# A two-layer attention and SwiGLU kernel: output projection over 448 rows in place of 512, and the second projection's banks, buffers and order

## The chip, the cores and the metric

The kernel runs on one core of a Trainium2 chip. The metric is the device time of one execution in microseconds (us), taken as the median of several runs. The core's engines appear in the profile as PE (the matmul engine, TensorE), PEld (its weight loads), DVE (VectorE), ACT (ScalarE), POOL (GpSimd) and SP (SyncE, which here only issues DMAs). A trailing q, as in SPq, is an engine's queue of DMA issues.

## The reference

Sequence length 2048, model width D = 448, 16 query heads of 28, one key and value head shared by all of them, and a feed-forward width of 1792. The same weights are used in both layers.

```python
def _A_ref(x, wq, wk, wv, wo):
    q = (x @ wq).reshape(B, S, 16, 28).transpose(0, 2, 1, 3)
    k = x @ wk
    v = x @ wv
    p = softmax(einsum("bhqd,bkd->bhqk", q, k) * 28 ** -0.5)
    o = einsum("bhqk,bkd->bhqd", p, v)
    return o.transpose(0, 2, 1, 3).reshape(B, S, 448) @ wo

def _B_ref(x, w_gate, w_up, w_down):
    return (silu(x @ w_gate) * (x @ w_up)) @ w_down

x = x + _A_ref(layernorm(x));  x = x + _B_ref(layernorm(x))   # layer 0
x = x + _A_ref(layernorm(x));  x = x + _B_ref(layernorm(x))   # layer 1
```

All inputs and the output are float32.

## The kernel before

**Precision.** Nearly every product of weights and activations is made in three matmuls: each operand is split into a rounded high part and the rest (names that end in h and l), and hi x hi, hi x lo and lo x hi are summed in PSUM. `split(h, l, r)` does it on POOL: L135 writes the high part and L136 the rest.

**Tiling.** The 2048 tokens are 4 chunks of 512, and a chunk has 4 token tiles of 128. The residual stream `xres` stays in SBUF. The 16 heads are 4 groups g of 4; in a group each head has 32 partitions, 28 used and 4 spare.

**Projection.** An object for the layer walks through 16 products (chunk c, slice m of the q, k, v weights), numbered by `seen`. Each is a run of matmuls into one PSUM bank (L312) that `bank(...)` deals out in the order of a tuple: before, `ALL` is banks 4 to 7 and then 0 to 3. ACT copies the bank to a stage buffer (L531), and SP sends that to DRAM (`qd`, `kt`), from where heads are read back in another layout. `plan[n, k]` lists what is written into the program around product n: for layer 0, the layer norm of the next chunk. A norm is, per token tile, BN statistics and their aggregate on DVE (L217, L218), for the chunk one reciprocal root on POOL (`scale`, L222 and L223), and per token tile the scaled rows on DVE (L230) with a copy on POOL (L232); PE flips those rows (L248) into the layout of the products. `maxima(c)` makes, with 4 matmuls (L439), a transposition (L441), a reduction and further small DVE steps, bounds on the scores of chunk c, which are taken off before the exponential. In the second layer the normed rows of chunks 0 to 2 come turned, by way of DRAM, and are split by ACT (L292) and DVE (L293, L302); chunk 3 is normed here (`ready`).

**Attention loop.** 128 cycles m in each layer; 8 of them (u = 0 to 7) make one (chunk, head group) i. A cycle has on PE the scores of two key tiles, y0 and y1 (L597): for each tile 3 passes of 4 matmuls with 32 rows, for j = 0 to 3 the heads of the group. j < 3 goes to three banks side by side (`three`), j = 3 to a single bank (`bank`). ACT takes the exponential of `three` (L619), DVE copies `bank` to a buffer `pair` (L618), and ACT takes the exponential of both tiles' copies at once (L620). Then PE makes P-V for the cycle before (L652) into the single bank of y0, and DVE adds it to an accumulator (L661). `singles` alternates banks 6 and 7 between y0 and y1.

**After the last cycle of a group**, `post` sends the sums of the exponentials (a row of ones in V gives them as the 29th row of each head) to `rs` (L675). `rest`, written into cycle m + 4, takes their reciprocals, sends them to DRAM and back as a broadcast (L686), and POOL multiplies (L693) and splits the result into `onh` and `onl`.

**Output projection.** `on` holds a chunk's four groups of 128 partitions, so the contraction is over 512 rows, 448 of them used; the weights `woh`, `wol` have the same layout, with zeros in the spare rows. When the last group of a chunk is through, 48 matmuls (4 token tiles x 4 groups x 3 parts, L582) are written behind cycle u = 6 of the next group, tiles 1, 2, 3 into the banks of `three` and tile 0 into a single bank, with an add to `xres` for each (L586): three adds behind tile 3 and one behind tile 0. This happens for chunks 0, 1 and 2 inside the loop, six times in all; for chunk 3 it stands behind the loop, among the first matmuls of the feed-forward part (`unit`, L332).

**Order.** Each engine takes its own instructions in the order in which the program was written. So where a piece is written (the tables `plan`, `due` and `aside`, and the place in `scores`) sets the order of every queue; engines wait for each other by semaphores. POOL also splits feed-forward weights (`weights`, L130 to L136 and L159) that are loaded in cycles u = 4 of groups 11 to 14. A slower variant of the whole (`full=True`) stands in a branch that is not taken with these inputs.

## Time and profile before

| | |
|---|---|
| median of 3 runs | 1984.87 us (1984.5 to 1985.03) |
| profiled execution | 1986.38 us, its span 1984.7 us |
| PE busy | 1960.1 us, 99% |
| ACT busy | 1270.1 us, 64% |
| DVE busy | 968.9 us, 49% |
| POOL busy | 555.3 us, 28% |
| mean granted TensorE clock | 0.996 |

The span is the time from the first to the last instruction of the profiled execution; the rest of its time lies around it. A row of a timeline gives the start in us from the span's start, the duration, the engine, the line and operation, out<-in, shapes and the number of equal instructions put together; in brackets is the idle time of the engine ahead of it, and what ended that. A row of the waits reads: engine and work, what it waited for, us in total, number of times, longest. A row of the chain of waits has the start, the length and the work. A row of a window gives its length, then busy time and instructions of PE, PEld, DVE, ACT and POOL, the granted clock (1 is full), the DMA engines' share and GB/s. Matmuls are pipelined: the step from one start to the next is what a matmul costs PE, and its own duration is longer. In the names, a trailing number of a buffer is left out.

Layer 0's projection lies at 9 to 70 us, its attention loop after that to about 540 us, the feed-forward part to 1001 us; the second projection at 1001 to 1054 us, with the second layer's attention and feed-forward behind it.

### The profile page before, as it was taken

What the parts mean: (1) busy time and instruction counts of PE and PEld (TensorE: products, weight loads), DVE (VectorE), ACT (ScalarE), POOL (GpSimd) and SP (SyncE); (2) the same over time, 40 slices, a digit from 0 to 9 for tenths busy, and PEclk for the clock granted to TensorE, in tenths of its full rate; (3) what the DMA queues carried; (4) which work ended last, traced back from release to release, by engine and by line L of the source; (5) the groups of instructions that cost most, each with busy time, mean ns of one, the idle gap of its engine ahead of it and who ended that gap; (6) DMA issues with size and microseconds to landing.
All of it is one profiled execution on the core that took longest, in us unless ns stands there. A gap on an engine that the chain in (4) does not pass through costs nothing. (4 is left out here: it accounts for less than half of the span.)

```text
span 1984.7 us, 43786 instructions
## 1 busy us (share of the span) xinstructions
PE 1960.1 (99%) x18469; PEld 1337.4 (67%) x18469; DVE 968.9 (49%) x1638; ACT 1270.1 (64%) x1888; POOL 555.3 (28%) x597
## 2 busy tenths in 40 slices
PE   9999999999999999999999999999999999999998
PEld 7544545445468999999974445454454789988886
DVE  6656565665743223222665565656657432222222
ACT  4899797997953333333348997979979433333332
POOL 5222113122214333333331221122221242333320
PEclk9999999999999999999999999999999999999999
DMA  5101011021030011110241010200211301011102
GB/s 165 54 23 33 18 36 39 19 54 31 24 84 26 17 32 32 32 32 22 79 134 35 26 31 12 62 12 23 51 48 26 74 17 32 17 31 32 32 1 76
DMA packets 99875, 80.50 MB, mean 41 GB/s; under 512 B 25848, under 2 KB 82296, under 8 KB 99672
## 3 DMA queue, kind: packets, MB, share of 16 engines
q1 hardware_dynamic: 98120, 76.44, 14.2%
q8 instruction: 146, 2.39, 0.5%
q10 hardware_dynamic: 1552, 1.20, 0.2%
q14 instruction: 57, 0.47, 0.1%
HBM read 56.24 MB, written 20.58 MB: 39 GB/s over the span
## 5 line engine op out<-in xcount | busy, mean ns | idle before, releaser
L619 ACT ACTIVATE pt<-three 128x1536 f32<-128x1536 f32 x512 | 714.9, 1449 | 65.7 <-PE three L597 62.4
L652 PE MATMUL bank<-pt,vsb 128*32 128x512 f32 x3072 | 490.8, 598 | 1.9 <-DVE pair L618 1.2
L652 PE MATMUL bank<-pair,vsb 128*32 128x512 f32 x1024 | 487.4, 598 | 0.5 <-ACT pair L620 0.5
L597 PE MATMUL bank<-qstack,keys 32*128 32x512 f32 x1536 | 471.9, 426 | 1.7 <-DVE xres L586 1.7
L332 PE MATMUL bank<-xh,wgh 64*128 64x512 f32 x1728 | 448.7, 389 | 0.0
L597 PE MATMUL three<-qstack,keys 32*128 32x512 f32 x4608 | 430.4, 409 | 2.5 <-ACT stage L531 2.5
L597 PEld LDWEIGHTS three<-qstack,keys 32*128 32x128 f32 x4608 | 262.8, 183 | 232.2 <-issue 203.0
L618 DVE COPY pair<-bank 128x512 f32<-128x512 f32 x512 | 353.8, 691 | 100.7 <-PE bank L597 71.6
L332 PE MATMUL bank<-xh,wgl 64*128 64x512 f32 x1404 | 370.3, 390 | 0.0
L332 PE MATMUL bank<-xl,wgh 64*128 64x512 f32 x1296 | 336.5, 389 | 0.0
L332 PE MATMUL bank<-wdh,h 64*128 64x448 f32 x1792 | 333.6, 363 | 1.7 <-ACT h L945 0.8
L944 DVE TENSOR_TENSOR sg<-bank,sg 128x512 f32<-128x512 f32 x112 | 77.4, 691 | 502.8 <-ACT sg L943 498.6
L332 PEld LDWEIGHTS bank<-xh,wgh 64*128 64x128 f32 x1728 | 265.7, 184 | 16.6 <-issue 1.3
L652 PEld LDWEIGHTS bank<-pt,vsb 128*32 128x32 f32 x3072 | 101.7, 109 | 253.2 <-issue 153.2
L620 ACT ACTIVATE pair<-pair 128x1024 f32<-128x1024 f32 x256 | 271.8, 1062 | 0.0
L597 PEld LDWEIGHTS bank<-qstack,keys 32*128 32x128 f32 x1536 | 245.1, 184 | 37.0 <-DVE o L659 5.2
L827 POOL TENSOR_TENSOR xres<-stage,xres 128x448 f32<-128x448 f32 x108 | 127.3, 1197 | 502.8 <-ACT stage L826 502.5
L332 PEld LDWEIGHTS bank<-wdh,h 64*128 64x128 f32 x1792 | 247.3, 184 | 15.2 <-issue 2.0
L661 DVE TENSOR_TENSOR o<-bank,o 128x512 f32<-128x512 f32 x224 | 154.7, 691 | 209.1 <-PE bank L652 209.1
L339 ACT COPY seen<-bank 128x1 f32<-128x1 f32 x664 | 82.1, 163 | 250.6 <-PE bank L332 247.6
L332 PEld LDWEIGHTS bank<-xh,wgl 64*128 64x128 f32 x1404 | 218.7, 184 | 14.1
L332 PE MATMUL bank<-wdl,h 64*128 64x448 f32 x896 | 221.1, 367 | 0.0
(133 smaller groups left out, 2120.9 us busy)
## 6 DMA issues: line engine op xcount, KB each, us to landing
o<-rd SPq DMA_DIRECT2D x32, 256.0 KB
qd<-stage SPq DMA_DIRECT2D x32, 224.0 KB
qraw<-qd SPq DMA_DIRECT2D x128, 56.0 KB
wdr<-in_B_w_down_dram SPq DMA_DIRECT2D x28, 224.0 KB
xt<-tb SPq DMA_DIRECT2D x24, 224.0 KB
wr<-in_B_w_gate_dram SPq DMA_DIRECT2D x28, 192.0 KB
wr<-in_B_w_up_dram SPq DMA_DIRECT2D x28, 192.0 KB
xn<-xt SPq DMA_DIRECT2D x6, 768.0 KB
```

Source lines behind the costliest of these rows:

```text
L332: nc.tensor.matmul(po, a, b, start=start, stop=stop, skip_group_check=True)
L339: nc.scalar.copy(seen[:, i : i + 1], po[:, 0:1])
L597: nc.tensor.matmul(three[:, j, :] if j < 3 else one, k[js, kp, ks], q[js, part, :], start=(z == 0), stop=(z == 2), tile_position=(32 * j, 0),)
L618: copies.append(nc.vector.tensor_copy(pt1, one))
L619: es.append(nc.scalar.activation(pt, threes[y], AF.Exp, scale=SCALE))
L620: es.append(nc.scalar.activation(pair, pair, AF.Exp, scale=SCALE))
L652: nc.tensor.matmul(to[32 * j : 32 * j + 32, :], vsb[:, n % NT, :], pts[n][j], start=(y == 0), stop=(y == 1), skip_group_check=True,)
L661: f = nc.vector.tensor_tensor(accs[i][:, 0, :], to, accs[i][:, 0, :], ALU.add)
L827: nc.gpsimd.tensor_tensor(r, s, r, ALU.add)
L944: nc.vector.tensor_tensor(in_order(sg, sq), natural(pg[1], sq), in_order(sg, sq), ALU.mult)
```

## The change

It has several parts.

1. **448 rows.** Heads 2 and 3 of group 0 (56 rows of the contraction) are moved into the 4 spare partitions of the other groups' heads (3 groups x 16 spare partitions = 48) and of group 0's own heads 0 and 1 (8). Groups 1 to 3 are then full, and group 0 has 64 rows. That half group is stored twice, in partitions 0 to 63 and in 64 to 127, so that two token tiles can use the two halves of the array side by side. `load_wo` loads the weights into this layout with 32 DMAs a layer in place of 8, and POOL's two zero fills go.
2. **Projection.** 36 matmuls over 128 rows for groups 1 to 3 and 12 over 64 rows, as 6 pairs: tiles 1 and 2, then 3 and 0. All four adds stand behind, in the order 1, 2, 3, 0. Behind the loop the pairs are tiles 0 and 1, then 2 and 3.
3. **Moving the rows.** `post` gives three pieces. `rest` (cycle m + 4) ends with the product on POOL. `spread` (m + 5) moves rows with DMAs on SP: for group 0, two writes to DRAM, two reads and one copy of the half group; for the others four reads of 4 rows. `parts` (m + 6, or m + 7 for group 0) does the split into `onh` and `onl`. The sums are sent with one DMA in place of four. For the last group of all, `rest` is written ahead of `unit(0, 0, 0)`, `spread` behind it, then the fetch of weights, then `parts`.
4. **Score order.** For even tiles (y0) the matmuls of a pass go j = 3, 0, 1, 2.
5. **Layer 0's projection.** The statistics and the root of chunks 2 and 3 are made together, ahead of chunk 2's scaled rows; POOL's root takes 8 columns.
6. **Second projection.** Its banks go round in the order 0 to 7; chunk 3's raw products use slices of a spare tile `xn` in place of two stage buffers; the norm of chunk 3 is applied behind product 5 in place of product 8.
7. **Last maxima.** Everything behind the transposition is written one cycle later.

The core of the diff:

```diff
-        fs = [lambda t=t: stat(t) for t in range(4)] + [scale]
+        fs = [lambda t=t: stat(t) for t in range(4 * chunks)] + [scale]
...
-            raw = self.pool.tile([P, 512], F32, name="stage")
+            if self.layer and c == NC - 1:
+                if "xn" not in self.spare:
+                    self.spare["xn"] = pers.tile([P, 4, 512], F32, name="xn")
+                raw = self.spare["xn"][:, self.seen % 4, :]
+            else:
+                raw = self.pool.tile([P, 512], F32, name="stage")
...
-            wide.append(ALL)
+            wide.append((0, 1, 2, 3, 4, 5, 6, 7) if self.layer else ALL)
...
+                    for g in (2 * z, 2 * z + 1):
+                        s_ = r[:, g % 2, :]
+                        if g == 0:
+                            for half in (0, 64):
+                                for q in range(2):
+                                    p0 = half + 32 * q
+                                    nc.sync.dma_start(s_[p0 : p0 + DH, :], wo[DH * q : DH * q + DH, :])
+                                    n0 = 4 * DH - 8 + 4 * q
+                                    nc.sync.dma_start(s_[p0 + DH : p0 + 32, :], wo[n0 : n0 + 4, :])
+                            continue
+                        own = wo[4 * DH * g : 4 * DH * g + 4 * DH, :]
+                        n0 = 2 * DH + 16 * g - 16
+                        for q in range(4):
+                            nc.sync.dma_start(s_[32 * q : 32 * q + DH, :], own[DH * q : DH * q + DH, :])
+                            nc.sync.dma_start(s_[DH + q :: 32, :], wo[n0 + 4 * q : n0 + 4 * q + 4, :])
                     zs = slice(2 * z, 2 * z + 2)
...
+                def passes(c):
+
                     oh, ol = on[c]
-                    ts_ = slice(P * t, P * t + P)
+                    return (oh, woh), (oh, wol), (ol, woh)
+
+                def add_to(c, t, po):
+
+                    return lambda: nc.vector.tensor_tensor(
+                        xres[:, 4 * c + t, :], po[:, 0:D], xres[:, 4 * c + t, :], ALU.add
+                    )
+
+                def full_rows(c, t, po, gs):
+
                     for g in gs:
-                        for z, (a, b) in enumerate(((oh, woh), (oh, wol), (ol, woh))):
+                        for z, (a, b) in enumerate(passes(c)):
                             nc.tensor.matmul(
-                                po[:, 0:D], a[:, g, ts_], b[:, g, :], start=(g + z == 0), stop=(g == NG - 1 and z == 2)
+                                po[:, 0:D], a[:, g, P * t : P * t + P], b[:, g, :],
+                                start=(g == 1 and z == 0), stop=False, skip_group_check=True,
                             )
...
+                def half_rows(c, ts, pos):
+
+                    for z, (a, b) in enumerate(passes(c)):
+                        for t, po, rs in zip(ts, pos, (slice(0, 64), slice(64, 128))):
+                            nc.tensor.matmul(
+                                po[:, 0:D], a[rs, 0, P * t : P * t + P], b[rs, 0, :],
+                                start=False, stop=(z == 2), skip_group_check=True,
+                            )
...
-                        for j in range(4):
+                        for j in (0, 1, 2, 3) if n % 2 else (3, 0, 1, 2):
...
+                    pos = [one, *(threes[0][:, n, :] for n in range(3))]
+                    for two in ((1, 2), (3, 0)):
+                        for t in two:
+                            full_rows(c, t, pos[t], range(1, NG))
+                        half_rows(c, two, [pos[t] for t in two])
+                    for t in (1, 2, 3, 0):
+                        add_to(c, t, pos[t])()
...
-                        due[m + 4] = post(i)
+                        rest, spread, parts = post(i)
+                        due[m + 4], due[m + 5], due[m + (7 if i % NG == 0 else 6)] = rest, spread, parts
...
+                        nc.gpsimd.tensor_tensor(rb, oraw, rb, ALU.mult)
+
+                    def spread():
+                        if g == 0:
+                            moved[c] = dram.tile([2 * DH, 512], F32, name=f"moved{self.layer}_{c}")
+                            for q in (0, 1):
+                                nc.sync.dma_start(moved[c][DH * q : DH * q + DH, :], rb[64 + 32 * q : 64 + 32 * q + DH, :])
+                            for q in (0, 1):
+                                n0 = 2 * DH - 8 + 4 * q
+                                nc.sync.dma_start(rb[32 * q + DH : 32 * q + 32, :], moved[c][n0 : n0 + 4, :])
+                            nc.sync.dma_start(rb[64:128, :], rb[0:64, :])
+                            return
+                        n0 = 16 * g - 16
+                        for q in range(4):
+                            nc.sync.dma_start(rb[DH + q :: 32, :], moved[c][n0 + 4 * q : n0 + 4 * q + 4, :])
+
+                    def parts():
                         oh, ol = on[c]
-                        nc.gpsimd.tensor_tensor(rb, oraw, rb, ALU.mult)
                         split(oh[:, g, :], ol[:, g, :], rb)
...
                 ff.unit(0, 0, 0)
-                due.popitem()[1]()
+                due.pop(min(due))()
                 ff.fetch(2)
+                due.pop(min(due))()
                 ff.unit(0, 0, 1)
...
+                c, pos = NC - 1, [bank(LOW)[1] for _ in range(4)]
+                for t in range(4):
+                    full_rows(c, t, pos[t], range(1, NG - 1))
+                while ff.left:
+                    ff.left.pop(0)()
+                for two in ((0, 1), (2, 3)):
+                    for t in two:
+                        full_rows(c, t, pos[t], range(NG - 1, NG))
+                    half_rows(c, two, [pos[t] for t in two])
+                for t in range(4):
+                    add_to(c, t, pos[t])()
...
-                a.plan[8, 0] = [ready]
+                a.plan[5, 1] = [ready]
...
-        fs, got = norm_steps(c)
+        fs, got = norm_steps(c, chunks=2 if c == 2 else 1)
         n = 4 * c - 4
-        at.plan[n, 1] = fs[:5]
-        at.plan[n + 1, 1] = fs[5:] + [lambda c=c, got=got: at.norms.__setitem__(c, got)]
+        if c == 2:
+            two = got
+            at.plan[n, 1] = fs[:9]
+        elif c == 1:
+            at.plan[n, 1] = fs[:5]
+        else:
+            at.plan[n, 1] = [lambda got=got: got.__setitem__("r", two["r"][:, 4:8])]
+        at.plan[n + 1, 1] = fs[-4:] + [lambda c=c, got=got: at.norms.__setitem__(c, got)]
```

The order of POOL around the product of chunk 2's last group (`o`, then its halves `onh` and `onl`; `wgh` to `wdl` are halves of feed-forward weights), before:

```order
137 L693 TENSOR_TENSOR o_4685<-o_4685 128x512
138 L135 TENSOR_SCALAR onh<-o_4685 128x512
139 L136 TENSOR_TENSOR onl<-o_4685,onh 128x512
140 L135 TENSOR_SCALAR wgh<-wr 128x1024
141 L136 TENSOR_TENSOR wgl<-wr,wgh 128x1024
142 L135 TENSOR_SCALAR wdh<-wdr 128x448
143 L136 TENSOR_TENSOR wdl<-wdr,wdh 128x448
```

and now:

```order
133 L729 TENSOR_TENSOR o_4717<-o_4717 128x512
134 L135 TENSOR_SCALAR wgh<-wr 128x1024
135 L136 TENSOR_TENSOR wgl<-wr,wgh 128x1024
136 L135 TENSOR_SCALAR wdh<-wdr 128x448
137 L136 TENSOR_TENSOR wdl<-wdr,wdh 128x448
138 L135 TENSOR_SCALAR onh<-o_4717 128x512
139 L136 TENSOR_TENSOR onl<-o_4717,onh 128x512
```

The four weight splits stood behind the halves of the quotient, and now they stand ahead of them.

The order of DVE in layer 0's projection, at the norm of chunk 2 (`stats`, `mv`: statistics; `rstd`: the root that POOL gives; `xn`: the scaled rows), before:

```order
43 L217 BN_STATS stats<-xres 128x6
44 L218 BN_AGGR mv<-stats 128x2 [waits DVE_49]
45 L230 TENSOR_SCALAR xn<-xres,mv,rstd 128x448 [waits Pool_49]
46 L230 TENSOR_SCALAR xn<-xres,mv,rstd 128x448 x2
47 L230 TENSOR_SCALAR xn<-xres,mv,rstd 128x448 [waits DVE_49]
```

and now:

```order
44 L218 BN_AGGR mv<-stats 128x2 [waits DVE_49]
45 L217 BN_STATS stats<-xres 128x6 [waits DMAHW2_49]
46 L218 BN_AGGR mv<-stats 128x2 [waits DVE_49]
47 L217 BN_STATS stats<-xres 128x6
48 L218 BN_AGGR mv<-stats 128x2 [waits DVE_49]
49 L217 BN_STATS stats<-xres 128x6
50 L218 BN_AGGR mv<-stats 128x2 [waits DVE_49]
51 L217 BN_STATS stats<-xres 128x6
52 L218 BN_AGGR mv<-stats 128x2 [waits DVE_49]
53 L230 TENSOR_SCALAR xn<-xres,mv,rstd_419 128x448 [waits Pool_49]
54 L230 TENSOR_SCALAR xn<-xres,mv,rstd_419 128x448 x3
```

The rows from the wait for DMAHW2 on are the statistics of chunk 3; the scaled rows of chunk 2 wait for POOL behind them.

The order of PE at the end of an output projection and the beginning of the next scores (`three`: the three banks side by side, `bank_79`: a single bank, `qstack`, `keys`: operands of the scores), before:

```order
995 L582 MATMUL bank_79<-woh,onh 128x448
996 L582 MATMUL bank_79<-wol,onh 128x448
997 L582 MATMUL bank_79<-woh,onl 128x448
998 L597 MATMUL three_797<-qstack_101,keys_98 128x512 [waits DVE_49]
999 L597 MATMUL three_797<-qstack_101,keys_98 128x512 x2
1000 L597 MATMUL bank_79<-qstack_101,keys_98 128x512 [waits DVE_49]
```

and now:

```order
983 L612 MATMUL bank_79<-woh,onl 128x448
984 L621 MATMUL three_794<-woh,onh 128x448
985 L621 MATMUL bank_79<-woh,onh 128x448
986 L621 MATMUL three_794<-wol,onh 128x448
987 L621 MATMUL bank_79<-wol,onh 128x448
988 L621 MATMUL three_794<-woh,onl 128x448
989 L621 MATMUL bank_79<-woh,onl 128x448
990 L633 MATMUL bank_79<-qstack_101,keys_98 128x512 [waits DVE_49]
991 L633 MATMUL three_794<-qstack_101,keys_98 128x512 x3
```

The single bank's matmuls end the projection in both; the next scores begin with `three` before, and now with the single bank, which waits for DVE.

The order of PE in the second projection, from the end of the eighth product to the ninth (one bank holds a product; `xh`, `xl` are the halves of the normed rows, `wh`, `wl` those of the weights). Before, the first maxima, a few rows ahead, use `bank_79`:

```order
6596 L312 MATMUL bank_6393<-xh,wh 128x512
6597 L312 MATMUL bank_6393<-xh,wl 128x512
6598 L312 MATMUL bank_6394<-xh,wh 128x512 [waits Activation_49]
6599 L312 MATMUL bank_6394<-xl,wh 128x512 [waits DVE_49]
6600 L312 MATMUL bank_6394<-xh,wl 128x512
6601 L312 MATMUL bank_6394<-xh,wh 128x512 [waits Activation_49]
```

and now, where the first maxima use `bank_6436`:

```order
6574 L312 MATMUL bank_6435<-xh,wh 128x512
6575 L312 MATMUL bank_6435<-xh,wl 128x512
6576 L312 MATMUL bank_6436<-xh,wh 128x512 [waits DVE_49,Activation_49]
6577 L312 MATMUL bank_6436<-xl,wh 128x512
6578 L312 MATMUL bank_6436<-xh,wl 128x512
6579 L312 MATMUL bank_6436<-xh,wh 128x512 [waits Activation_49]
```

The ninth product now uses the bank of the maxima and waits for DVE there.

79 lines of the change are left out of this document (31 added, 48 removed).

## The prediction

> **What bounds the kernel now.** I read the page first, then the waits of the matmul engine, then the chain of waits and the timeline at each place that the change touches.
>
> ```profile
> PE 1960.1 (99%) x18469; PEld 1337.4 (67%) x18469; DVE 968.9 (49%) x1638; ACT 1270.1 (64%) x1888; POOL 555.3 (28%) x597
> PE three L597 <- ACT stage L531: 2.5, 2, 2.2
> PE bank L312 <- DVE xres L823: 2.2, 1, 2.2
> PE bank L248 <- POOL xn L232: 1.9, 1, 1.9
> PE bank L597 <- DVE xres L586: 1.7, 6, 0.3
> PE bank L652 <- DVE pair L618: 1.2, 1, 1.2
> ```
>
> PE is busy 99% of the span of 1984.7 us. So the change can win only PE steps and the few waits listed, and it loses wherever PE is made to wait. The second to fourth rows are waits in the second projection (three of 2.2, 2.2 and 1.9 us), the fifth the six seams behind the output projection, the last the start of attention in layer 0.
>
> **Output projection, matmuls.** The chain of waits around one of the six in the attention loop:
>
> ```profile
> 1191.52 7.50 PE three L582 x36
> 1199.02 2.44 PE bank L582 x12
> 1201.48 0.64 DVE xres L586
> ```
>
> 48 matmuls take 9.94 us, 0.205 each. Half-row matmuls of the same 448 columns stand in the tail, in the timeline of PE:
>
> ```profile
> 1562.30 0.37 PE L332 MATMUL bank<-wdl,h 64*128 64x448 f32 x2
> 1562.50 0.57 PE L332 MATMUL bank<-wdh,h 64*128 64x448 f32 x4
> 1563.12 0.37 PE L332 MATMUL bank<-wdh,h 64*128 64x448 f32 x2
> 1563.42 0.47 PE L582 MATMUL bank<-woh,onh 128*128 128x448 f32 x1
> 1563.72 0.36 PE L582 MATMUL bank<-wol,onh 128*128 128x448 f32 x1
> ```
>
> Two side by side advance PE by 0.20 us (1562.30 to 1562.50), like one full matmul. From 1563.12 over 1563.42 to 1563.72 PE passes from half rows to full rows: two steps of 0.30, so a change of mode costs 2 x 0.095 = 0.19. In a loop projection 12 full matmuls go (-2.46) and 6 pairs come (+1.23). Full, half, full, half, scores has three changes more than full, scores: +0.57. Net -0.66 each, -4.0 for six. At the tail two changes more in each layer: -1.23 + 0.38 = -0.85, twice -1.7. Matmuls together: -5.7. The extra weight DMAs and the removed POOL fills count nothing: they are issued two or three head groups, of eight cycles each, ahead of the first projection, under the scores; without that cover each DMA would cost some 0.46 of SP (four in 1.84, below).
>
> "TensorEngine Tiling (Array Packing)" of the Trainium skill, Tiling Modes, Key Properties, says that changing the mode, not just the tile, drains TensorE. The rows above agree, with 0.19 us; without the drain the term would be -9.8.
>
> **The seam.** Before, the first score matmul of `bank` waited for the one add of 1201.48 (0.3 in each of six by the waits above, with three others free to go). Now two adds (tiles 3 and 0) wait for the last pair, tile 0's second, and j=3, which needs its bank, stands first. One add more (0.62 to 0.64) less some overlap: +0.6 each, +3.6 for six.
>
> **Late halves.** POOL split the quotient into onh and onl directly behind its product. Now SP's spread DMAs lie between, and at chunk 2 also four splits of feed-forward weights:
>
> ```profile
> 202.63 1.27 POOL L693 TENSOR_TENSOR o<-o 128x512 f32<-128x512 f32 x1 [7.64 <-DMA o<-rd]
> 204.71 1.28 POOL L136 TENSOR_TENSOR onl<-o,onh 128x512 fp32r<-128x512 f32 x1
> 207.16 0.47 PE L582 MATMUL three<-woh,onh 128*128 128x448 f32 x1
> 1173.89 1.84 SPq L421 DMA_DIRECT2D qraw<-qd  x4
> 1177.39 0.62 POOL L135 TENSOR_SCALAR qstack<-qraw 128x512 fp32r<-128x512 f32 x1 [8.45 <-DMA qraw<-qd]
> 458.72 1.29 POOL L693 TENSOR_TENSOR o<-o 128x512 f32<-128x512 f32 x1 [9.50 <-DMA o<-rd]
> 462.06 1.05 POOL L135 TENSOR_SCALAR wgh<-wr 128x1024 fp32r<-128x1024 f32 x1
> 466.22 1.15 POOL L136 TENSOR_TENSOR wdl<-wdr,wdh 128x448 fp32r<-128x448 f32 x1
> 462.35 0.47 PE L582 MATMUL three<-woh,onh 128*128 128x448 f32 x1
> 1443.41 1.29 POOL L693 TENSOR_TENSOR o<-o 128x512 f32<-128x512 f32 x1 [9.77 <-DMA o<-rd]
> 1446.65 0.47 PE L582 MATMUL three<-woh,onh 128*128 128x448 f32 x1
> ```
>
> Four such DMAs take 3.5 us from the first issue to the POOL work that they release (1173.89 to 1177.39). So at chunk 0 onl comes at 202.63 + 1.27 + 3.5 + 2.1 (the two splits) = 209.5. The ninth matmul needs it 0.30 + 7 x 0.205 = 1.73 after 207.16, at 208.89: about 0.5 late, for two chunks in two layers +2.0 (0 if the DMAs land 0.5 sooner, 4 if they take 0.5 longer). At chunk 2 the weight splits run from the product's end, 460.1, for the 5.3 us that they took before (462.06 to 467.37), then onh and onl until 467.5, against 462.35 + 1.73 = 464.1: 3.4 late. In layer 1 the quotient comes 3.24 ahead of the matmuls instead of 3.63, so 3.7. Together +7.1. What is queued behind is covered by scores: on SP, behind the spread DMAs that wait for the product, the loads of the next queries; on POOL, behind the splits that wait for them, the splits of those queries, a head group ahead of their use. At the tail the first feed-forward unit's matmuls stand between product and split: nothing, or at most chunk 0's 0.5 again.
>
> **Layer 0's projection.**
>
> ```profile
> 31.29 0.59 DVE L217 BATCH_NORM_STATS2 stats<-xres 128x6 f32<-128x448 f32 x1
> 31.92 0.18 DVE L218 BATCH_NORM_AGGREGATE mv<-stats 128x2 f32<-128x6 f32 x1
> 32.54 1.01 POOL L223 TENSOR_TENSOR rstd<-rstd,halfn 128x4 f32<-128x4 f32 x1
> 33.59 1.78 DVE L230 TENSOR_SCALAR xn<-xres,mv,rstd 128x448 f32<-128x448 f32 x4 [1.49 <-POOL rstd L223]
> 35.02 1.18 PE L248 MATMUL bank<-ident,xn 128*128 128x128 f32 x8
> ```
>
> The flips at 35.02 follow the chain stats, root, scaled rows at once. Chunk 3's four statistics (0.73 apart, 2.9) now stand inside it, and the root is 8 wide: 1.01 for 4, so 1.01 to 2.02. The flips come 2.9 to 3.9 later, and no PE work is left ahead of them. Chunk 3's own turn then has one statistic chain less in DVE's queue, worth between nothing and one of its steps of 0.6. So +2.3 to +3.9, and I take the middle, +3.1.
>
> **Second projection.**
>
> ```profile
> 1004.72 0.50 PE L312 MATMUL bank<-xh,wh 128*128 128x512 f32 x1 [2.24 <-DVE xres L823]
> 1016.16 0.50 PE L312 MATMUL bank<-xh,wh 128*128 128x512 f32 x1 [0.21 <-ACT xh L292]
> 1018.78 0.72 DVE L441 STREAM_TRANSPOSE sg<-bank 128x512 f32<-128x512 f32 x1
> 1028.73 0.85 PE L248 MATMUL bank<-ident,xn 128*128 128x128 f32 x4 [1.90 <-POOL xn L232]
> 1030.00:1040.00 10.00, 10.00 (x39) 8.04 (x38) 4.83 (x8) 5.72 (x11) 4.37 (x11) 0.83 0.52 153
> 1040.00:1060.00 20.00, 17.63 (x133) 9.93 (x131) 9.76 (x18) 12.41 (x13) 8.06 (x15) 0.83 0.24 72
> ```
>
> The last two rows are windows; the third number from the end is the granted clock. Banks 0 to 7 in order let the first matmul go without the add (-2.2); rows normed early free the flips (-1.9); spare tiles for chunk 3's raw rows free the last ACT copies, so that the second score tile hardly waits (-2.2). Against that, the ninth product now shares its bank with the first maxima, whose transposition (1018.78) stands in DVE's queue behind the splitting of chunk 2's turned rows, which come from a DMA; the ninth product needs the same rows, and at 1016.16 PE already waited 0.21 for them. If that DMA is not sooner, PE, at this place by 1013.7 (1016.16 less 2.2 and the 0.2), stands until the transposition ends at 1019.5: +5.8. A bank used again at the fourteenth product costs some 1.4 (between 0 and the 2.2 of the waits above). The clock of .83 over 10 and over 20 us cost 1.7 + 3.4 = 5.1 us, behind the wait at 1028.73 and the one at the second score tile; both go, and one stretch of 1.7 follows the new stall. With 0.5 for the later second half of the last maxima: -6.3 + 5.8 + 1.4 - 5.1 + 1.7 - 0.5 = -3. The range is -10 (the new stall away with its clock) to +2 (the clock not back).
>
> **Small terms.** Deferring the last maxima in layer 0 removes the wait of 1.2: -1. The score order: P-V starts at the end of a copy of y0's fourth bank, and PE is ready at almost the same time:
>
> ```profile
> 302.44 0.40 PE L597 MATMUL three<-qstack,keys 32*128 32x512 f32 x3
> 302.45 0.39 PE L597 MATMUL bank<-qstack,keys 32*128 32x512 f32 x1
> 302.92 0.69 DVE L618 COPY pair<-bank 128x512 f32<-128x512 f32 x1 [0.22 <-PE bank L597]
> 303.67 0.63 PE L652 MATMUL bank<-pt,vsb 128*32 128x512 f32 x3
> ```
>
> Now j=3 takes the place of 302.44 instead of 302.45: 0.012 in each of some 250 cycles, -3, between 0 (PE itself not ready sooner) and -6 (another 0.012 in the same queue).
>
> **The clock after new stalls.** A wait of 1.90 at 1028.73 was followed by a clock of .83 over 10 us, a loss of 1.7; one of 2.24 ahead of 1004.72 was not. Two stalls of 3.5 at chunk 2: I take one drop, +1.7, between 0 and 3.4. "TensorE: Matmul & The Clock Gate" (the Trainium skill), Part 1, gives half rate after an idle window of about 3.4 us, free-running. By it both stalls at the threshold could drop, and the waits of 1.9 and 2.2 should not have; the trace disagrees on those. The drop after both is a case below.
>
> **Sum.** -5.7 + 3.6 + 2.0 + 7.1 + 3.1 - 3 - 1 - 3 + 1.7 = +4.8 us. The profiled execution took 1986.38 (1.68 outside its span), so 1991.2; it lies 1.51 above the median of 1984.87. Against that median 1989.7, rounded to 1990.
>
> **Rivals.** *Not slower: the new stall at the ninth product is not there.* If chunk 2's DMAs, issued earlier because PE's first wait is gone, let that splitting end by 1013.7, 5.8 and the clock's 1.7 vanish and the projection gives -10.5: -2.7 in all, 1982.2. It decides from a gain of 5 us there. For it speaks that SP's issues partly follow PE; against it the 0.21 at 1016.16, which shows that already before the turned rows of chunk 2 came last, behind DMAs and not behind PE. With the score order at its good end it is 1979.2.
> *More clock loss.* Half clock follows every stall of 3 us: both at chunk 2 (+1.7) and layer 0's (+1.7), and the root takes its full 2.02 (+0.8): 1993.9. For it speak the low clocks after waits of 1.9 and 2.2, against it 1004.72.
> *The pairs do not run side by side.* Then 6 pairs cost 12 steps, +1.23 for each of eight projections: 1999.5. Against it stand the tail's rows of 64x448, two in 0.2 us.
>
> **How the numbers follow.** The sum as worked out 0.53, the missing stall 0.28, more clock loss 0.14, no side by side 0.05. A difference under 0.2%, 4 us, can hardly be told from no change. The missing stall at 1982.2, with the score order's end at 1979.2, is faster by more in half of its chance (0.15) and within in the other (0.13). The sum's own range, its terms' ends added as if independent, is 1982 to 1996: of its chance 0.05 lies below 1981, 0.06 within, 0.42 above. The other two are slower. So faster 0.20, within 0.19, slower 0.61. The range for 8 in 10 takes in most of the missing stall and the extra clock loss: 1980 to 1998.
>
> **What would show it.** Right: 36 full and 6 pairs of matmuls at 0.2 us with four steps of 0.3 in each projection; an idle of 3 to 4 us inside the third of each layer, released by POOL onl; the flips of chunk 2 in layer 0 waiting 3 us for rows; no wait for xres at the start of the second projection, and one for the first maxima's transposition near its ninth product. Wrong: chunk 2's halves ready in time, a steady cycle that moves by more than 0.03 us from 3.65 (each 0.01 is 2.5 us), or another work queued ahead of the splits on POOL or SP than counted.

## The result and the profile after

The changed kernel took 2001.4 us (median of 6 runs, 1998.46 to 2006.54) against 1984.95 us before: a ratio of 1.0084, 95% interval 1.0071 to 1.0097. It is slower by 16.5 us; the forecast was slower by 4.8, and the time lies above the range of 1980 to 1998. The profiled execution took 2002.02 us, with a span of 2000.3 and a mean clock of 0.990. The kernel before was timed again beside every set of experiments, at 1984.8 to 1985.6 us, so their times are compared with 2001.4 directly.

Taking the two profiled executions apart at the same places of the program shows where the 15.6 us between the spans come from (a loop projection is counted from its first matmul to the first P-V behind it, so with its seam; layer 0's feed-forward part is counted to the first matmul of the second projection, at 981 us before, and its last matmuls run on among that projection's):

| stage | before | after | difference | forecast |
|---|---|---|---|---|
| layer 0, start to first score | 63.84 | 68.40 | +4.6 | +3.1 |
| layer 0, first score to first projection | 143.3 | 141.5 | -1.8 | -1 and order |
| six loop projections with their seams | 74.7 | 101.5 | +26.8 | +8.7 and one clock drop of 1.7 |
| cycles between and behind them | 645.8 | 646.5 | +0.7 | part of the order's -3 |
| behind each loop, to the end of the last projection (two) | 45.8 | 44.5 | -1.3 | -1.7 |
| feed-forward parts, both | 800.7 | 792.2 | -8.5 | 0 |
| second projection, to the first projection of layer 1 | 210.5 | 205.7 | -4.8 | -3 |

The waits of PE in the changed kernel, the costliest first:

```profile
PE bank L633 <- DVE xres L604: 14.3, 6, 2.4
PE three L612 <- POOL onh L135: 6.2, 3, 3.2
PE bank L312 <- DVE sg L440: 5.7, 1, 5.7
PE bank L248 <- DVE xn L230: 4.1, 2, 2.5
PE three L612 <- POOL onl L136: 4.1, 6, 0.7
```

The first row is the seam: 1.7 us in six waits before, 14.3 now. Its place in the timeline of PE and DVE, at the first projection:

```profile
215.53 0.38 PE L621 MATMUL three<-woh,onl 64*128 64x448 f32 x2
220.21 0.36 PE L621 MATMUL three<-woh,onl 64*128 64x448 f32 x1
220.68 1.69 DVE L604 TENSOR_TENSOR xres<-three,xres 128x448 f32<-128x448 f32 x3 [9.97 <-PE three L621]
222.28 0.61 DVE L604 TENSOR_TENSOR xres<-bank,xres 128x448 f32<-128x448 f32 x1
222.95 0.49 PE L633 MATMUL bank<-qstack,keys 32*128 32x512 f32 x1 [2.38 <-DVE xres L604]
223.00:227.00 4.00, 4.00 (x36) 1.62 (x40) 1.39 (x2) 3.01 (x3) 0.00 (x0) 0.67 0.00 0
```

The adds of tiles 1 and 2, whose products had ended nearly 5 us earlier (the first row), start only with the last matmul of tile 3, and DVE was idle for 9.97 us ahead of them. All four stand in a row, the one that j = 3 needs comes last, and behind the wait the granted clock (third number from the end of the window's row) is .67 over 4 us.

Chunk 2 on POOL in layer 0, with the matmul that waits and the clock behind it:

```profile
468.38 1.30 POOL L729 TENSOR_TENSOR o<-o 128x512 f32<-128x512 f32 x1 [11.86 <-DMA o<-rd]
470.33 1.04 POOL L135 TENSOR_SCALAR wgh<-wr 128x1024 fp32r<-128x1024 f32 x1 [0.65 <-DMA wr<-in_B_w_up_dram]
474.45 1.13 POOL L136 TENSOR_TENSOR wdl<-wdr,wdh 128x448 fp32r<-128x448 f32 x1
475.55 0.62 POOL L135 TENSOR_SCALAR onh<-o 128x512 fp32r<-128x512 f32 x1
476.22 0.47 PE L612 MATMUL three<-woh,onh 128*128 128x448 f32 x1 [3.17 <-POOL onh L135]
480.00:484.00 4.00, 4.00 (x14) 2.73 (x13) 0.00 (x0) 0.00 (x0) 0.00 (x0) 0.53 0.00 0
```

This is as forecast, but that PE waits first for onh (3.17) and then 0.7 for onl, and the clock is at half behind it, here for 6.8 us. Layer 0's norm and the second projection:

```profile
35.51 1.64 POOL L223 TENSOR_TENSOR rstd<-rstd,halfn 128x8 f32<-128x8 f32 x1
37.18 1.78 DVE L230 TENSOR_SCALAR xn<-xres,mv,rstd 128x448 f32<-128x448 f32 x4 [2.13 <-POOL rstd L223]
37.75 3.36 PE L248 MATMUL bank<-ident,xn 128*128 128x128 f32 x16 [2.54 <-DVE xn L230]
1031.99 0.72 DVE L440 STREAM_TRANSPOSE sg<-bank 128x512 f32<-128x512 f32 x1
1032.86 0.76 PE L312 MATMUL bank<-xh,wh 128*128 128x512 f32 x1 [5.72 <-DVE sg L440]
1032.00:1036.00 4.00, 3.15 (x8) 2.50 (x9) 3.53 (x7) 0.91 (x2) 0.69 (x3) 0.50 0.16 49
```

The root over 8 columns took 1.64, the wait 2.54; the new stall in the second projection 5.72, with half clock behind it.

The feed-forward part of layer 0 in windows, of the kernel before and then of the changed one. The x in brackets behind the busy time of PE counts its matmuls:

```profile
590.00:980.00 390.00, 389.79 (x3510) 375.99 (x3511) 131.30 (x208) 131.56 (x484) 139.21 (x125) 1.00 0.11 31
```

```profile
608.00:994.00 386.00, 385.56 (x3516) 379.74 (x3514) 132.41 (x208) 129.54 (x484) 138.92 (x125) 1.00 0.11 31
```

About the same matmuls, at full clock in both, with PE idle for less than 0.5 us, take 4 us less: 0.1098 us each in place of 0.1111. Nothing in the forecast had a term for that.

### The profile page after: what moved, and what is told of

It reads as the page before. It is cut to its first block, busy times and chain, and to the rows that moved or that the text cites. A ratio compares the mean times of both kernels' runs of the same rounds, so it can differ in the third digit from the quotient of the medians.

```text
span 2000.3 us, 43996 instructions
## 1 busy us (share of the span) xinstructions
PE 1951.9 (98%) x18469; PEld 1333.9 (67%) x18469; DVE 967.2 (48%) x1638; ACT 1261.0 (63%) x1888; POOL 550.5 (28%) x591
## 4 chain that ended last, share of the span: by engine, by line
PE 82%; ACT 9%; DMA 3%; DVE 2%; POOL 1%; SPq 1%; issue 1%; ACTq 0%; POOLq 0%; DVEq 0%
PE bank L332 39%; PE bank L689 17%; PE bank L633 13%; ACT pt L655 6%; PE bank L312 4%; PE three L633 4%; ACT pair L656 2%; PE three L612 1%; PE bank L612 1%; DMA o<-rd 1%; DVE xres L604 1%; PE three L621 1%; PE bank L248 0%; DMA rd<-rs 0%; POOL onl L136 0%
## 5 line engine op out<-in xcount | busy, mean ns | idle before, releaser
L655 ACT ACTIVATE pt<-three 128x1536 f32<-128x1536 f32 x512 | 725.1, 1491 | 93.7 <-PE three L633 93.7
L633 PE MATMUL bank<-qstack,keys 32*128 32x512 f32 x1536 | 476.2, 427 | 14.3 <-DVE xres L604 14.3
L332 PE MATMUL bank<-xh,wgh 64*128 64x512 f32 x1728 | 413.4, 387 | 0.0
L332 PE MATMUL bank<-xh,wgl 64*128 64x512 f32 x1404 | 346.1, 386 | 0.0
L332 PE MATMUL bank<-wdh,h 64*128 64x448 f32 x1792 | 324.5, 362 | 1.4 <-ACT h L1005 0.8
L332 PE MATMUL bank<-xl,wgh 64*128 64x512 f32 x1296 | 309.5, 386 | 0.0
L656 ACT ACTIVATE pair<-pair 128x1024 f32<-128x1024 f32 x256 | 283.2, 1106 | 0.0
L633 PEld LDWEIGHTS three<-qstack,keys 32*128 32x128 f32 x4608 | 263.6, 184 | 12.4 <-ACT stage L539 0.7
L332 PEld LDWEIGHTS bank<-xh,wgh 64*128 64x128 f32 x1728 | 233.1, 184 | 13.3 <-DVE sg L1004 0.7
L332 PEld LDWEIGHTS bank<-wdh,h 64*128 64x128 f32 x1792 | 223.3, 183 | 12.7 <-issue 2.0
L332 PE MATMUL bank<-wdl,h 64*128 64x448 f32 x896 | 203.1, 364 | 0.0
L332 PEld LDWEIGHTS bank<-xh,wgl 64*128 64x128 f32 x1404 | 194.8, 184 | 11.5
```

The lines of the kernel that those rows point to most:

```text
L332: nc.tensor.matmul(po, a, b, start=start, stop=stop, skip_group_check=True)
L633: nc.tensor.matmul(three[:, j, :] if j < 3 else one, k[js, kp, ks], q[js, part, :], start=(z == 0), stop=(z == 2), tile_position=(32 * j, 0),)
L655: es.append(nc.scalar.activation(pt, threes[y], AF.Exp, scale=SCALE))
L656: es.append(nc.scalar.activation(pair, pair, AF.Exp, scale=SCALE))
```

## The experiments

The theory after this comparison: the seam costs 2.1 us more of idle in each of six places and a stretch of low clock behind most of them; POOL's queue costs the stall at chunk 2; the two projections' stalls cost what was worked out; and something that is not in the written order of the work makes the feed-forward parts faster. The rivals are in the expectations.

**Adds behind their pair.**

```diff
-                    pos = [one, *(threes[0][:, n, :] for n in range(3))]
-                    for two in ((1, 2), (3, 0)):
+                    pos = [one, threes[0][:, 0, :], threes[0][:, 1, :], threes[1][:, 0, :]]
+                    for two in ((1, 2), (0, 3)):
...
-                    for t in (1, 2, 3, 0):
-                        add_to(c, t, pos[t])()
+                        for t in two:
+                            add_to(c, t, pos[t])()
```

> The changed kernel, but tile 3's product goes into the three banks of y1, and the adds of a pair are written right behind that pair: tiles 1 and 2 during the second half, then tile 0, then tile 3. Theory (all four adds wait for the last matmul into the shared banks, and the first score matmul for the fourth add): the idle ahead of the first scores falls from 2.4 us to 0.7 in each of six seams, with less low clock behind it: 10 us less than the changed kernel, about 1991.5. Rival (the seam is paid by the last pair itself or by the score order, not by the queue of adds): the idle stays at 2 us or more and the time within 3 us of 2001.4.

Measured: 1984.35 us, 17 less. The seam in the timeline, and its row in the waits of PE:

```profile
220.39 1.16 DVE L604 TENSOR_TENSOR xres<-three,xres 128x448 f32<-128x448 f32 x2 [5.14 <-PE three L621]
224.96 0.62 DVE L604 TENSOR_TENSOR xres<-bank,xres 128x448 f32<-128x448 f32 x1 [3.41 <-PE three L621]
225.50 0.61 DVE L604 TENSOR_TENSOR xres<-three,xres 128x448 f32<-128x448 f32 x1
225.64 0.50 PE L633 MATMUL bank<-qstack,keys 32*128 32x512 f32 x1 [0.71 <-DVE xres L604]
PE bank L633 <- DVE xres L604: 4.3, 6, 0.7
```

Two adds ran during the second half, and the idle fell from 2.38 to 0.71. In the profiled execution the six projections take 12.4 us less than in the changed kernel's, 10.0 of it this idle, and the cycles behind them 4.2 less, since low clock is left only at chunk 2's stalls. (Its span is just 12.7 us shorter, because a wait of 3.2 us of PE for ACT near the start of the program, at a place that the edit doesn't touch, and more low clock there put its first scores 4.6 us later.) The theory holds, and more was to be had than expected, because five of the six seams had drawn a low clock.

**Weights behind the halves.**

```diff
-                    if u == 4 and 10 < i <= 11 + FG:
+                    if u == (6 if i == 12 else 4) and 10 < i <= 11 + FG:
```

> The changed kernel, but the feed-forward weights of group 12 are loaded and split two cycles later, behind the halves of the quotient. Theory (POOL's four weight splits hold the halves back, and the clock falls behind that stall): the waits of PE for onh of 3.2 and 2.8 us at chunk 2 go to about 0.2, as at chunk 1, and the third projection of each layer becomes as short as the second: 8 us less, about 1993.5. Rival (the halves are late by their DMAs, and POOL's queue only shows it): the waits for onh stay over 1.5 us, less than 3 us gained.

Measured: 1990.37 us, 11 less. POOL at chunk 2 of layer 0:

```profile
464.86 1.28 POOL L729 TENSOR_TENSOR o<-o 128x512 f32<-128x512 f32 x1 [10.92 <-DMA o<-rd]
469.87 0.62 POOL L135 TENSOR_SCALAR onh<-o 128x512 fp32r<-128x512 f32 x1 [3.72 <-DMA o<-moved]
473.51 1.05 POOL L135 TENSOR_SCALAR wgh<-wr 128x1024 fp32r<-128x1024 f32 x1 [1.67 <-DMA wr<-in_B_w_up_dram]
```

The waits for onh are gone from the list; those for onl (0.7, six times) stay. Chunk 2's projection takes 14.8 us in layer 0 in place of 21.7, and 15.8 in layer 1 in place of 19.1. The theory holds.

**Everything one cycle earlier.**

```diff
-                        due[m + 4], due[m + 5], due[m + (7 if i % NG == 0 else 6)] = rest, spread, parts
+                        due[m + 3], due[m + 4], due[m + (6 if i % NG == 0 else 5)] = rest, spread, parts
```

> The changed kernel, but the reciprocal with its product, the moving of rows and the split are each written one cycle (3.65 us) earlier. Theory (the DMAs between product and split make the halves late by under 1 us at chunks 0 and 1): the waits for onh and onl go at these four projections, 0.7 to 0.9 us each, and the one at chunk 2 stays, since the weight splits still stand ahead: 2 to 4 us less, about 1998.5. Rival (writing it earlier does not move the product, which waits for the sums): the time within 1.5 us of 2001.4.

Measured: 2004.78 us, 3 more, against an expected gain of 2 to 4. The waits for onl fell from 4.1 to 0.5 in all, but the longest for onh, at chunk 2, grew from 3.2 to 6.0:

```profile
PE three L612 <- POOL onh L135: 11.3, 2, 6.0
PE bank L633 <- DVE o L696: 3.1, 4, 1.3
463.50 2.10 SPq L743 DMA_DIRECT2D o<-moved  x4
469.79 0.59 SPq L159 DMA_DIRECT2D wdr<-in_B_w_down_dram  x1
471.51 1.05 POOL L135 TENSOR_SCALAR wgh<-wr 128x1024 fp32r<-128x1024 f32 x1 [6.07 <-DMA wr<-in_B_w_up_dram]
476.68 0.62 POOL L135 TENSOR_SCALAR onh<-o 128x512 fp32r<-128x512 f32 x1
```

The spread DMAs now stand ahead of the weights' in SP's queue and wait there for the product until 463.50; so the weights land later, POOL waits 6 us for them, and the halves stand behind. A second new wait, 3.1 us, came from the DVE steps that moved with it. The expectation had looked at POOL's queue and not at SP's.

**Layer 0's statistics a chunk at a time.**

```diff
-        fs, got = norm_steps(c, chunks=2 if c == 2 else 1)
+        fs, got = norm_steps(c)
...
+        at.plan[n, 1] = fs[:5]
+        at.plan[n + 1, 1] = fs[5:] + [lambda c=c, got=got: at.norms.__setitem__(c, got)]
```

> The changed kernel, but in layer 0's projection the statistics and roots of chunks 2 and 3 are made one chunk at a time, as before. Theory (the four statistics of chunk 3 and the wider root stand inside the chain to chunk 2's flips): the wait of 2.5 us and the low clock behind it go, layer 0's first scores start 4.5 us sooner: about 1997. Rival (the time is the moved norm's own, and comes back at chunk 3): under 1.5 us less.

Measured: 2006.83 us, 5 more. The first scores do start 4.2 us sooner (64.23 against 68.40 us), so the chain is what was thought; but the feed-forward parts are long again, 390.7 and 409.6 us from the last projection to their ends against 386.5 and 405.7. Their row, for layer 0:

```profile
604.00:994.00 390.00, 389.55 (x3514) 376.22 (x3510) 132.15 (x209) 132.00 (x484) 139.17 (x125) 1.00 0.11 31
```

This was the clue to the term that no theory had. Without the root tile of 8 columns (64 bytes a partition in its two buffers), everything allocated behind it should stand at the addresses of the kernel before. So the next run put only such a tile into the kernel before.

**64 spare bytes in the kernel before.**

```diff
             got["r"] = rstd
+            if c == 2:
+                pers.tile([P, 8], F32, name="pad", bufs=2)
```

> The kernel before, with nothing but an unused spare tile of 64 bytes a partition, where the changed kernel has its wider root: all tiles allocated behind it (feed-forward weights and operands among them) move up by 64 bytes, as they do in the changed kernel. Theory (the feed-forward part's 4.2 and 4.3 us a layer that the changed kernel gained come from that shift alone): both feed-forward parts shorten by 4 us, 8 us less, about 1977. Rival (they come from how the half-row pairs of the new output projection enter the feed-forward part, or vary between executions): the time within 1.5 us of before.

Measured: 1976.41 us, ratio 0.9954 (0.9938 to 0.9971) to the kernel before. The instructions are the same; the feed-forward row:

```profile
590.00:977.00 387.00, 386.78 (x3519) 379.36 (x3517) 132.85 (x210) 129.39 (x484) 138.62 (x125) 1.00 0.11 31
```

Both feed-forward parts shorten by 4 us. Together with the run before this one, in which the changed kernel lost that gain, it shows that its 8.5 us came from where its tiles happen to lie.

**128 spare bytes**, the same edit with 16 columns:

> The kernel before with an unused spare tile of 128 bytes a partition in place of 64. If the feed-forward steps follow the address in steps of 64 out of 128 bytes, they are back at the long ones: 1985. If any shift away from the old place helps: about 1976.5, as with 64.

Measured: 1977.8 us (0.9941 to 0.9975 of before), with layer 0's feed-forward row as short:

```profile
594.00:979.00 385.00, 384.75 (x3512) 374.31 (x3510) 131.66 (x207) 129.21 (x484) 138.72 (x125) 1.00 0.12 31
```

So 128 bytes do as 64, and it isn't a matter of every second place. Which tile's address counts, and why, stays open.

**The score order undone.**

```diff
-                        for j in (0, 1, 2, 3) if n % 2 else (3, 0, 1, 2):
+                        for j in range(4):
```

> The changed kernel with the scores' order j = 0, 1, 2, 3 for even tiles as before. Theory (j = 3 first takes 0.046 us off the start of the copy and 0.018 off the cycle of 3.648): the median cycle goes back to 3.648 and the time rises by 4 to 5 us, to about 2006; the idle at the seams stays near 2.4, since the scores' other matmuls wait for the same adds. Rival (the order is worth 0.01 a cycle or nothing): less than 2 us.

Measured: 2005.9 us, 4.5 more. The median cycle is 3.649 us, against 3.630 in the changed kernel and 3.648 before. At the seam the three shared banks now wait first, for three adds in place of four:

```profile
PE three L633 <- DVE xres L604: 11.1, 6, 1.8
```

That is 3.2 us less idle than the changed kernel's 14.3, so the expectation for the seam was wrong. In the two profiled executions the cycles outside the projections differ by only 1.9 us, where 250 cycles of 0.018 would make 4.5; in some cycles, those with the small DVE steps and those behind a seam, nothing is gained. The order is worth 2 to 5 us.

**The second projection's banks as before.**

```diff
-            wide.append((0, 1, 2, 3, 4, 5, 6, 7) if self.layer else ALL)
+            wide.append(ALL)
```

> The changed kernel with the second projection's banks in the order of before (4 to 7, then 0 to 3). Theory (the wait of 5.7 us for the first maxima's transposition, and the low clock of 3.4 us behind it, are the price of the new order, which saves only the wait of 2.2 for the add): 5 to 7 us less than 2001.4, about 1995.5. Rival (chunk 2's rows come late in any order, so the wait only changes its name): under 2 us less.

Measured: 1995.96 us, 5.4 less. In its waits the row of 5.7 for `sg` is gone, and the add's wait is back:

```profile
PE bank L312 <- DVE xres L883: 2.2, 1, 2.2
```

From the start of the second projection to layer 1's first score the profiled execution takes 61.1 us, against 64.3 in the changed kernel, so 3.2 of the 5.4 us are found there. The rival falls: nothing takes the place of the wait of 5.7 us, so chunk 2's rows were not what was late. The gain is at the low end of what was expected.

**Adds behind their pair, with tile 3 left in the shared banks.**

```diff
-                    for two in ((1, 2), (3, 0)):
+                    for two in ((1, 2), (0, 3)):
...
-                    for t in (1, 2, 3, 0):
-                        add_to(c, t, pos[t])()
+                        for t in two:
+                            add_to(c, t, pos[t])()
```

> The changed kernel with the adds of a pair behind that pair and tile 0 ahead of tile 3, but tile 3 still in the three shared banks. If an add waits for the last matmul written ahead of it into the shared banks, tiles 1 and 2 are added during tile 0's matmuls, and the seam's idle is the two adds that are left, 1.3 us in place of 2.4. If it is the add's own place in DVE's queue or anything else of the pair, it stays at 2.4.

Measured: 1987.34 us in a single run, 14 less than the changed kernel. DVE and PE around the first seam:

```profile
215.98 1.16 DVE L604 TENSOR_TENSOR xres<-three,xres 128x448 f32<-128x448 f32 x2 [5.11 <-PE three L621]
220.55 0.62 DVE L604 TENSOR_TENSOR xres<-bank,xres 128x448 f32<-128x448 f32 x1 [3.41 <-PE three L621]
221.23 0.50 PE L633 MATMUL bank<-qstack,keys 32*128 32x512 f32 x1 [0.71 <-DVE xres L604]
221.76 0.50 PE L633 MATMUL three<-qstack,keys 32*128 32x512 f32 x3
```

Written ahead of tile 3's matmuls, the adds of tiles 1 and 2 start 4.6 us ahead of the others. So an add waits for the last matmul that is written ahead of it into the shared banks, whichever of them that fills. The seam is 0.71 and then 0.53 more until `three` starts, 1.2 in all, as expected.

**Five repairs at once**: adds, weights, statistics with 64 spare bytes kept, and banks, as above.

> The changed kernel with five repairs at once: the adds of a pair behind that pair (tile 3 in the other banks), the weights of group 12 two cycles later, layer 0's statistics a chunk at a time with the spare 64 bytes kept, and the second projection's banks as before. If the causes are separate and add up (12 + 11 + 4 + 6 us): about 1968, faster than before by 0.8%. If they cover the same time (low clock counted twice, waits that come back elsewhere): 1974 to 1980.

Measured: 1966.99 us, 0.9909 (0.9892 to 0.9926) of before. The causes add up but for 3 us: as measured one by one (17, 11, 4.2 and 5.4 us), they would have given 1964. What is left of waits for the new projection:

```profile
PE bank L635 <- DVE xres L606: 4.3, 6, 0.7
PE three L614 <- POOL onl L136: 3.9, 6, 0.7
```

**The repairs with 512 rows.** The projection of before (load, 48 matmuls, adds, `post`) put back into that kernel:

```diff
-                    pos = [one, threes[0][:, 0, :], threes[0][:, 1, :], threes[1][:, 0, :]]
...
+                    adds = []
+                    for t in (1, 2, 3):
+                        adds.append(outproj(c, t, threes[0][:, t - 1, :]))
+                    for f in adds:
+                        f()
+                    outproj(c, 0, one)()
```

> The kernel with the five repairs, but with the 512-row output projection of before: weights with zero rows, 48 full matmuls, adds and split as before. All else of the change stays. Theory (matmuls and mode changes give back some 5.5 us, and the late onl of 0.65 and the seam with its add take as much): within 3 us of the repaired kernel's 1967, so that the 448 rows themselves are worth about nothing here. Rival (the half-row pairs are what makes the repaired kernel fast): 4 us or more slower than 1967.

Measured: 1965.76 us, against 1966.99 with 448 rows; the ranges of the runs overlap (1965.43 to 1967.06, and 1966.45 to 1968.48, in two sessions). So the 448 rows as repaired are worth nothing: what the matmuls save goes into mode changes and the late onl. The 18 to 20 us that both gained over the kernel before come from the rest, about 8 of them from the shifted addresses (both feed-forward parts are as short as in the changed kernel).

**The projection one cycle later.**

```diff
-                    if not todo or u != 6:
+                    if not todo or u != 7:
```

> The repaired kernel with the output projection written one cycle later (behind cycle u = 7 of the next group in place of 6), with everything ahead of it left in place. Theory (the remaining waits for onl, 0.65 each in six, are the DMAs between product and split): these waits go, 3.9 us less than 1967, about 1963. Rival (the wait only moves, to the sums of the group that ends at u = 7): within 1.5 us of 1967.

Measured: 1961.73 us, 0.9881 (0.9864 to 0.9897) of before, the fastest of all. The waits for onl are gone from the list, whose first row is the seam:

```profile
PE bank L635 <- DVE xres L606: 4.3, 6, 0.7
```

With the halves in time, the 448 rows are 4.0 us faster than 512 (1961.73 against 1965.76, measured together). In the two profiled executions a loop projection with its seam takes 11.9 us against 12.45. The 512 rows were not run one cycle later, but they have no waits for halves that this could have taken away. The change's idea pays, once nothing waits for it.

## Why the prediction was wrong

*Direction.* Right: slower, and in part for reasons that the forecast named; the stalls it listed were there, in their places. The size was missed: 16.5 us in place of 4.8.

*Matmuls (-5.7).* The pairs ran side by side at 0.2 us with steps of 0.3 at each change of mode; 448 rows against 512, free of waits, came to -4.0, so the term was somewhat too large.

*The seam (+3.6).* This is the step that failed. It said that two adds wait for the last pair and that one add more costs 0.6. All four wait, and the idle grew by 12.6 us instead of 3.6 (14.3 against 1.7). The profile before could have told:

```profile
214.37 0.36 PE L582 MATMUL three<-woh,onl 128*128 128x448 f32 x1
214.84 1.69 DVE L586 TENSOR_TENSOR xres<-three,xres 128x448 f32<-128x448 f32 x3 [6.84 <-PE three L582]
```

Of its three adds from the shared banks, none started before the last matmul into those banks, though tile 1 had long been done and DVE had been idle for 6.84 us. Writing the adds behind their pairs gave 17 us back with tile 3 in the other three banks, and 14 with tile 3 left where it was.

*The clock (+1.7).* Far too small, for the most part for the same reason. It took one drop for the two stalls at chunk 2, but waits of 2.4 us at the seams fell into the same class as the 1.90 and 2.23 us that had drawn a low clock before. Behind five of the six seams of the changed kernel a stretch of low clock follows; with the idle at 0.7 none did. By the clock's record in the two traces, matmuls at half clock lost 17.0 us in the changed kernel and 4.9 before: 8.5 behind the five seams, 4.8 at both stalls of chunk 2, 1.9 behind the new stall of the second projection and 1.7 behind layer 0's flips. So +12 stands against the forecast's -1.7 (+1.7 here, -5.1 + 1.7 in the second projection), which is a larger miss than the seam's idle itself. Inside the six projections, idle and waits for halves explain 12.6 + 10.3 of the 26.8 us and the matmuls about -4; the rest, some 8 us, is left for the part of the low clock that lies there.

*Late halves (+9.1).* Right: 10.3 us in all (6.2 for onh, 4.1 for onl), the stalls at chunk 2 of 3.2 + 0.7 and 2.8 + 0.7 against 3.4 and 3.7. PE stopped at onh, not at onl as forecast, because the weight splits hold back both.

*Layer 0's projection (+3.1).* Right in its mechanism: +4.6, the flips' wait 2.5, a root of 1.64, and 1.7 for low clock behind the wait, which the term had left to the rival. Taking it away gave 4.2 back.

*Second projection (-3).* Right in its main parts: the new stall 5.7 against 5.8, half clock behind it; the 1.4 for a bank used again at the fourteenth product is not among the waits; -4.8 in all up to the first projection of layer 1, where the score order has a part.

*Score order (-3).* Right by its size, wrong in its reason: the copy of the fourth bank starts about 0.05 us sooner in the cycle, not 0.012, and the cycle gains 0.018 of it; why no more wasn't tried. 2 to 5 us.

*Feed-forward.* Missing: the forecast put it at nothing, without a reason. Without the 8.5 us that the shifted addresses gave, the changed kernel would have been slower by about 25 us, so the real miss is larger than the totals show; that the time came out within 4 us of the range is luck.

Of the rivals, 1999.5 was nearest in number, but its mechanism is false: the pairs did run side by side. "More clock loss" (1993.9) was nearest in its mechanism, and it too lacked the seam.

## What to carry to other kernels

A consumer of one of several products in a shared tile can wait for the last write to the tile that is written ahead of it: write each consumer right behind its own product, or give the last products a tile of their own. Where an idle of PE of about 2 us may draw a low clock, count it twice, once for the wait and once for what runs slow behind it. When a work step is delayed or moved, read every queue that it passes, the DMA issues first; and before a gain or a loss is put down to an edit, see whether it moved the addresses of everything allocated behind it.

## What the runs showed of the hardware

A shift of 64 or 128 bytes a partition of the tiles behind one point made 64-row matmuls in pairs step about 1.1% faster over two feed-forward parts of 390 and 410 us, at full clock and with PE hardly idle: 8.4 us of 1985 with 64 bytes, 7.8 with 128, with not one instruction changed. In layer 0's part the two halves of the array start their matmuls more evenly in the changed kernel (0.09 and 0.14 us apart by turns, as medians) than in the kernel before (0.04 and 0.19). But in layer 1's part, which shortens as much, most pairs start nearly together in both kernels (0.004 and 0.20), so this spacing isn't what the gain hangs on.

In the changed kernel a low clock followed five of six idles of 2.4 us at the seams and every one of 2.5 us and more elsewhere; no run has one behind a seam of 0.7 us. Each stretch is at 0.5 and lasts 3.41 us, or 6.83 behind the longest stalls; one of 3.41 us under matmuls costs 1.7 us.

Which idles of about 2 us draw one can be read from the clock's record. All low stretches of an execution begin on one grid with steps of 3.413 us (in the changed kernel those at 224.37, 354.08 and 490.61 us are 38 and 40 steps apart). Six of the kernels (the changed one and the five runs on it that leave the adds together) have seams with an idle of 1.85 or 2.38 us, 36 in all. In 27 of them at least 1.79 us of the idle fell into one step, and the clock was low from the end of that step on. In the other 9 the idle lay across two steps with at most 1.66 us in either, and no stretch followed. The changed kernel's sixth seam, at 1478.55 us, is one of these, with 0.89 and 1.49 us:

```profile
1480.00:1484.00 4.00, 3.94 (x49) 1.71 (x48) 2.31 (x4) 4.00 (x4) 0.00 (x0) 1.00 0.00 0
```

So at the seams it is chance where an idle falls on the grid, and with it whether it costs 1.7 us more. Elsewhere this bound is not a sharp one. The wait for the add at the start of the second projection had no low clock in the kernel before (2.24 us, 1.64 of it in one step), but had one in the same kernel with 64 spare bytes (2.30 us, 1.51 in one step); and with the weights behind the halves, layer 0's idle of 2.55 us (1.76 in one step) had none.
